# Six group buffers for the bias, w_out's first words loaded in two earlier places, and their conversion spread over twelve slots

## The chip, the cores and the metric

The kernel runs on one core of a Trainium2 chip. The metric is the device time of one execution in microseconds; lower is better. A run's number is the median of several executions.

## The reference

Three layers are computed one after the other. The first is attention over 4 batches and 8 heads with 576 positions of 64 numbers, with a bias per pair of positions that a small network computes from the positions alone:

```python
scores = scale * np.matmul(q, k.transpose(0, 1, 3, 2))
x = (psi_rel / psi_i)[..., None]
h = np.maximum(x @ w1 + b1, 0.0)
bias = h @ w2
scores = scores + bias.transpose(2, 0, 1)[None, :, :, :]
...
attn = np.exp(scores)
attn = attn / (np.sum(attn, axis=-1, keepdims=True) + 1e-09)
return np.matmul(attn, v).astype(np.float32)
```

The second layer is a gated one, `(x @ w1) * (x @ w2) @ w3 @ w_out`, and the third a softmax-weighted one with a layer norm. The weights of the last two layers arrive as 64-bit floats and are made into 32-bit floats on the chip.

## The kernel before

**The bias.** `Bias.run` (L178 on) computes the bias of all heads in 36 groups of 16 query rows. For a group, four masks of 128 rows are made from a table of logarithms (`masks`, L163), about 11 of 16 on ScalarE (L169) and the others on VectorE (L171), two groups ahead. TensorE multiplies them into two PSUM halves (L192, 24 matmuls for a piece of up to 512 columns). VectorE combines the two halves into a row buffer `rs` in SBUF (L202 and L207), GpSimd writes the mirrored part of it (`pool_round`, L54), and SyncE's queue SP writes the buffer to DRAM (`write`, L47, 295.5 KB, shown as `bias_d<-rs`). There are three `rs` buffers (L199), so group n+3 waits in L202 until the write of group n has landed.

After each group, `beside(n)` puts other things between: the first pair's q and k are prepared (`Attention.start`), and bias rows are read back from DRAM for the attention (`load_bias`, shown as `b<-bias_d` and `bt<-bias_d`). At n = 23 the first two of the attention's bias blocks are read, and right after them `load_wo` loads 1 MB of `w_out` (two DMAs of 512 KB, `rwo<-in_wo`). All these DMAs are issued by SP in the order of the code; a write to DRAM stands behind whatever was issued before it.

**The attention.** It works in slots; ten slots make one pair of heads and one batch, and each engine's order in a slot is the order of the code in `slot` (L490 on). In slot s, VectorE adds the bias to the scores of block k of slot s-1 (`add_bias`, L389), takes reciprocals (L405) and makes the second half of transposed blocks (L512); ScalarE takes exponentials (L396) two slots behind and copies transposed blocks (L496); GpSimd adds to the sums (L403), normalises (L409), and splits the next pair's q, k and v into high and low parts (L54 and L57); TensorE makes scores (L376), transposes (L419) from slot 8 on, and values (L462) from slot 11 on. SP copies q and k into place for the next pair (`q<-qh`, `k<-kr`, L51).

**w_out's conversion.** `f64_steps` (L64 on) turns 64-bit words into floats in five steps: one on ScalarE (L69) and four on VectorE (L70 to L73). `first_wo` makes two such chains, each with a DMA at its end (`big<-wo`), twelve steps in all, in the order a1 b1 a2 b2 and so on. `FILL` (L223) says how many of them are taken at the end of which slot: two in slot 3, eight in slot 4, two in slot 5. The other parts of w_out are converted by `conv_wo`, thirteen slots for each (`wx`, `wraw`).

Of the kernel before, what the change touches and what calls it, by code (L numbers as in the profile page):

```python
# [7 lines left out]
F = mybir.dt.float32  # L8
B = mybir.dt.bfloat16
R = mybir.dt.float32r  # L10
U = mybir.dt.uint32
# [6 lines left out]
S = 576  # L18
# [65 lines left out]
class Bias:  # L84
# [93 lines left out]
    def run(self, beside):  # L178
        nc = self.nc
        order = list(range(32, 36)) + list(range(32))  # L180
        mq = [self.masks(g) for g in order[: self.AHEAD]]
        for n, g in enumerate(order):
            w, r = self.width(g), 16 * g + 15
            mk = mq.pop(0)
            pieces = [(0, w)] if w <= 512 else [(0, w // 2), (w // 2, w // 2)]
            made = []
            for at, ln in pieces:
                ps = self.pp.tile([128, 2, 512], F, tag="ps", name="ps")
                for ab in range(2):
                    for part in range(3):  # L190
                        for q in range(4):
                            nc.tensor.matmul(  # L192
                                ps[32 * q : 32 * q + 32, ab, :ln], self.cb[:, part, ab], mk[q][:, at : at + ln],
                                start=part == 0, stop=part == 2, tile_position=(0, 32 * q),
                            )
                made.append(ps)
            if n + self.AHEAD < len(order):
                mq.append(self.masks(order[n + self.AHEAD]))
            rs = self.wp.tile([128, 2 * S], F, tag="rs", name="rs", bufs=3)  # L199
            for (at, ln), ps in zip(pieces, made):  # L200
                to = rs[:, r + at : r + at + ln]
                nc.vector.scalar_tensor_tensor(  # L202
                    out=to, in0=self.lt[:, at : at + ln], scalar=self.ip16[:, g : g + 1], in1=ps[:, 0, :ln], op0=ALU.mult, op1=ALU.mult
                )
            for (at, ln), ps in zip(pieces, made):
                to = rs[:, r + at : r + at + ln]
                nc.vector.tensor_tensor(out=to, in0=to, in1=ps[:, 1, :ln], op=ALU.add)  # L207
            self.ch.pool_round(rs[:, :r], rs[:, r + 1 : 2 * r + 1][:, ::-1])
            self.write(g, rs)
            beside(n)  # L210
        nc.scalar.activation(self.warm, self.warm, AF.Exp)


class Attention:
# [5 lines left out]

    LAG = 8
    AVLAG = 2
    FILL = {3: 2, 4: 8, 5: 2}  # L223

    def __init__(self, ch, i, bias, x_d, ga):
        self.ch, self.nc, self.i = ch, ch.nc, i
# [23 lines left out]
        self.tps = ch.pool(self.psr, "atp", "right", bufs=2, space=PSUM)  # L250
        self.ops = ch.pool(self.psr, "aop", "right", bufs=1, space=PSUM)

    def load_wo(self):

        for f in range(2):
            self.ch.load(self.ga.raw_wo[:, f], self.i["wo"].bitcast(U)[f * 128 : f * 128 + 128])

    def first_wo(self):

# [230 lines left out]
    def slot(self, s):  # L490
# [33 lines left out]
        if n < NP:  # L524
# [19 lines left out]
            if s == 0:  # L544
                self.fill = self.first_wo()
            for _ in range(self.FILL.get(s, 0)):
                self.fill.pop(0)()
# [505 lines left out]
def tile_kernel(tc, i, out):  # L1053
    with tc.manual_schedule(), tc.tile_pool(name="dram", bufs=1, space=DRAM) as dp:
        x_d = [dp.tile([2, DM, S], F, name="x_d%d" % b) for b in range(NB)]
        x2_d = [dp.tile([DM, TC], F, name="x2_d%d" % c) for c in range(NC)]
        gw_d = dp.tile([FF, DM], F, name="gw_d")
        ch = Chip(tc)

        ga = Gated(ch, i, x_d, x2_d, gw_d)  # L1060
        ga.open_keep()
        bias = Bias(ch, i, dp)
        bias.open()
        at = Attention(ch, i, bias, x_d, ga)
        at.open_left()

        def beside(n):

            at.start(n)
            if n == 7:  # L1070
                at.load_bias(0, 0)
            if n == 23:
                at.load_bias(0, 1, 2)
                at.load_wo()
            if n == 26:
                at.load_bias(0, 5, 6)
            if n == 29:
                at.load_bias(0, 3)
                at.load_bias(0, 7)

        bias.run(beside)
        at.load_bias(0, 4)
        at.load_bias(0, 8)
        bias.ctx.close()
        at.open_right()
        scored = 10 * len(at.pairs)
        for s in range(at.slots()):
            n = s - scored
            if n == 0:
                at.left.close()  # L1090
                at.psl.close()
                ga.open_left()
            if n == ga.MID:
                at.top.close()
                ga.open_mid()
            at.slot(s)
            ga.early(n)
        at.right.close()
        at.psr.close()
        ga.open_right()  # L1100
        ga.run()
        ga.right.close()
        ga.psr.close()
        so = Solu(ch, i, ga, out)
        so.open()
        so.run()
        so.ctx.close()
        ga.left.close()
        ga.psl.close()
# [62 lines left out]
```

## Time and profile before

| | us |
|---|---|
| median of 3 runs | 978.24 |
| lowest and highest run | 974.11, 980.3 |
| the profiled execution's own time | 973.8 |
| its span, first to last instruction | 972.0 |

TensorE (PE) is busy 893.5 us of the span, VectorE (DVE) 602.2, ScalarE (ACT) 495.6 and GpSimd (POOL) 414.4. The mean granted TensorE clock is 0.979 of full speed. Times in the trace count from the span's start: the bias phase fills the first 84 us, the attention runs to about 400 us, and the two other layers fill the rest.

### The profile page before, as it was taken

The numbers are of one execution on the slowest core, as the hardware profiler recorded it, in microseconds if no ns is written. First come the engines' busy times: TensorE is split into PE (matmuls) and PEld (weight loads), VectorE is DVE, ScalarE is ACT, GpSimd is POOL, SyncE is SP. The second block draws the span as 40 slices with busy tenths as digits, with TensorE's granted clock in tenths as the row PEclk, the third lists the DMA queues.
The fourth block names the chain that finished last, engine by engine and source line by source line (L and its number), as shares of the span: only waits on it lengthen the run. The fifth ranks groups of instructions, "written<-read, shape, count | busy, mean of one in ns | idle before, by whom it ended". The sixth has DMA issues, their size and how long they took to land.

```text
span 972.0 us, 16454 instructions
## 1 busy us (share of the span) xinstructions
PE 893.5 (92%) x5890; PEld 792.3 (82%) x5890; DVE 602.2 (62%) x1292; ACT 495.6 (51%) x1018; POOL 414.4 (43%) x536
## 2 busy tenths in 40 slices
PE   5666999999989996799899999999999999999998
PEld 4334888888888885688799999999999888888886
DVE  7878889888888888899915656230111644444442
ACT  8974888788787886454423432332222333233222
POOL 3125887887877863010203657572322221022000
PEclk9987999999999998899999999999999999999999
DMA  4767789789789674555404252502110211111000
GB/s 139 252 226 215 210 219 276 212 233 288 191 227 304 178 194 147 160 191 178 157 18 159 74 192 87 178 18 86 35 65 24 62 49 55 31 46 55 22 23 33
DMA packets 83842, 133.76 MB, mean 138 GB/s; under 512 B 14896, under 2 KB 47536, under 8 KB 83760
## 3 DMA queue, kind: packets, MB, share of 16 engines
q1 hardware_dynamic: 83616, 132.40, 44.9%
q8 instruction: 47, 0.77, 0.3%
q10 hardware_dynamic: 144, 0.29, 0.1%
q14 instruction: 35, 0.29, 0.1%
HBM read 71.44 MB, written 31.86 MB: 106 GB/s over the span
## 4 chain that ended last, share of the span: by engine, by line
PE 57%; DVE 17%; POOL 9%; DMA 7%; issue 5%; ACT 3%; SPq 2%; POOLq 0%; DVEq 0%; ACTq 0%
PE ab L81 9%; PE ab L80 9%; PE ab L79 9%; PE o L81 3%; PE o L80 3%; PE o L79 3%; PE x L81 3%; PE x L80 3%; PE x L79 3%; PE op L462 2%; PE tp L419 2%; DVE e L389 2%; PE sp L376 2%; DVE etl L512 2%; PE ps L192 2%
## 5 line engine op out<-in xcount | busy, mean ns | idle before, releaser
L79 PE MATMUL ab<-xh,ab 128*128 128x384 f32 x384 | 130.8, 341 | 7.4 <-ACT ab L661 7.0
L81 PE MATMUL ab<-xh,ab 128*128 128x384 f32 x384 | 130.3, 339 | 0.9 <-DVE ab L664 0.9
L80 PE MATMUL ab<-xl,ab 128*128 128x384 f32 x384 | 130.4, 340 | 0.4 <-DVE xl L735 0.4
L771 DVE TENSOR_TENSOR a<-ab,a 128x384 f32<-128x384 f32 x48 | 26.7, 556 | 134.8 <-ACT a L770 134.8
L409 POOL TENSOR_SCALAR e<-e,st 128x576 f32<-128x576 f32 x128 | 96.2, 760 | 28.0 <-DVE st L405 27.0
L62 POOL TENSOR_TENSOR gl<-a,gh 128x384 fp32r<-128x384 f32 x40 | 46.0, 1150 | 142.2 <-ACT gh L61 142.2
L419 PE MATMUL tp<-idt,e 128*128 128x128 f32 x576 | 89.4, 278 | 18.6 <-DVE etl L512 15.4
L376 PE MATMUL sp<-k,q 128*128 128x288 f32 x512 | 95.8, 312 | 10.5 <-DVE st L389 8.3
L396 ACT ACTIVATE e<-e,st 128x576 f32<-128x576 f32 x128 | 100.0, 782 | 8.1 <-DVE st L389 7.9
L496 ACT CAST eth<-tp 128x512 fp32r<-128x512 f32 (+1 forms) x160 | 85.1, 543 | 35.9 <-PE tp L419 33.2
L512 DVE TENSOR_TENSOR etl<-tp,eth 128x512 fp32r<-128x512 f32 (+1 forms) x160 | 99.1, 627 | 5.3 <-ACT eth L496 4.3
L389 DVE CUSTOM_DVE_ANT_0 e<-sp,bt 128x576 f32<-128x576 f32 x128 | 95.4, 746 | 1.7 <-PE sp L376 1.7
L376 PEld LDWEIGHTS sp<-k,q 128*128 128x128 f32 x512 | 76.0, 194 | 19.4 <-DVE st L389 11.8
L419 PEld LDWEIGHTS tp<-idt,e 128*128 128x128 f32 x576 | 66.9, 141 | 28.8 <-DVE etl L512 13.2
L984 DVE TENSOR_REDUCE st<-ab 128x1 f32<-128x1024 f32 x18 | 22.0, 1224 | 107.8 <-PE ab L81 107.8
L1004 POOL TENSOR_TENSOR st<-st,half 128x1 f32<-128x1 f32 x18 | 9.9, 549 | 176.0 <-DVE st L1003 176.0
L79 PEld LDWEIGHTS ab<-xh,ab 128*128 128x128 f32 x384 | 73.1, 190 | 9.2 <-ACT ab L661 7.6
L770 ACT COPY a<-ab 128x384 f32<-128x384 f32 x48 | 22.9, 478 | 111.5 <-PE ab L81 96.1
L192 PE MATMUL ps<-mk,cb 128*32 128x264 bf16 (+17 forms) x1056 | 53.2, 347 | 27.4 <-DVE mk L171 18.0
L81 PEld LDWEIGHTS ab<-xh,ab 128*128 128x128 f32 x384 | 72.9, 190 | 2.3 <-DVE ab L664 2.3
L80 PEld LDWEIGHTS ab<-xl,ab 128*128 128x128 f32 x384 | 73.1, 190 | 1.5 <-DVE xl L735 1.3
L192 PEld LDWEIGHTS <-cb 128*32 128x32 bf16 x1056 | 32.7, 104 | 47.4 <-issue 23.9
(164 smaller groups left out, 2310.7 us busy)
## 6 DMA issues: line engine op xcount, KB each, us to landing
bias_d<-rs SPq DMA_DIRECT2D x36, 295.5 KB, 2.7
qkr<-in_qk SPq DMA_DIRECT2D x16, 608.0 KB, 4.6
k<-kr SPq DMA_DIRECT2D x32, 288.0 KB, 4.2
x_d<-o SPq DMA_DIRECT2D x64, 144.0 KB, 4.1
k<-kr SPq DMA_DIRECT2D x32, 256.0 KB, 4.2
raw<-in_w SPq DMA_DIRECT2D x16, 512.0 KB, 4.5
raw<-in_w3t SPq DMA_DIRECT2D x16, 512.0 KB, 4.1
vr<-in_v SPq DMA_DIRECT2D x16, 288.0 KB, 4.4
```

The costliest lines, as they stand in the source:

```text
L62: (eng or self.nc.gpsimd).tensor_tensor(out=lo, in0=x, in1=hi.bitcast(F), op=ALU.subtract)
L79: mm(out, a[0], b[0], start=first, stop=False)
L80: mm(out, a[0], b[1], start=False, stop=False)
L81: mm(out, a[1], b[0], start=False, stop=last)
L192: nc.tensor.matmul(ps[32 * q : 32 * q + 32, ab, :ln], self.cb[:, part, ab], mk[q][:, at : at + ln], start=part == 0, stop=part == 2, tile_ ...
L376: nc.tensor.matmul(ps[:, half, :HS], w["q"][:, h, q * 128 : q * 128 + 128], w["k"][:, h, x, half * HS : half * HS + HS], start=x == 0, sto ...
L389: self.nc.vector.tensor_tensor_reduce(out=halves(e), in0=ps[:, :, :HS], in1=halves(self.BT[(self.pairs[n][0], k)]), scale=-0.125, scalar=3e38,
L396: self.nc.scalar.activation(e, e, AF.Exp, bias=st[:, c : c + 1], scale=-1.0, accum_out=st[:, 2 + c : 3 + c])
L409: self.nc.gpsimd.tensor_scalar(out=e, in0=e, scalar1=st[:, c : c + 1], scalar2=1.0, op0=ALU.mult, op1=ALU.mult)
L419: tr = lambda c, src: nc.tensor.transpose(ps[: src.shape[1], c * 128 : c * 128 + 128], src, self.idt)
L496: self.nc.scalar.copy(hi, src)
L512: self.nc.vector.tensor_tensor(out=lo, in0=src, in1=hi.bitcast(F), op=ALU.subtract)
```

## The change

Three things are changed. The tag `rs` gets six buffers in place of three. `load_wo` takes one half at a time and is called after group 10 and after group 16 (the 11th and the 17th), no longer twice after group 23. `FILL` takes one of the twelve steps in each of the slots 0 to 11.

```diff
-            rs = self.wp.tile([128, 2 * S], F, tag="rs", name="rs", bufs=3)
+            rs = self.wp.tile([128, 2 * S], F, tag="rs", name="rs", bufs=6)
...
-    FILL = {3: 2, 4: 8, 5: 2}
+    FILL = {s: 1 for s in range(12)}
...
-    def load_wo(self):
+    def load_wo(self, f):
 
-        for f in range(2):
-            self.ch.load(self.ga.raw_wo[:, f], self.i["wo"].bitcast(U)[f * 128 : f * 128 + 128])
+        self.ch.load(self.ga.raw_wo[:, f], self.i["wo"].bitcast(U)[f * 128 : f * 128 + 128])
...
+            if n in (10, 16):
+                at.load_wo(n // 16)
             if n == 23:
                 at.load_bias(0, 1, 2)
-                at.load_wo()
```

On SP's queue, in the last two thirds of the bias phase, this stood before (`bias_d_74` and `bias_d_75` are two of the three DRAM areas of the bias, `rwo` is w_out's raw words, `bt` a bias block for the attention):

```order
L51 DMA k<-kr 64x2x64
L47 DMA bias_d_74<-rs 128x591 x3
L47 DMA qkr<-in_qk 128x1216
L47 DMA bias_d_74<-rs 128x591 x5
L47 DMA bias_d_75<-rs 128x591 x4
L47 DMA bt<-bias_d_74 128x2x576
L47 DMA rwo<-in_wo 128x1024 x2
L47 DMA bias_d_75<-rs 128x591 x3
```

Now there stands:

```order
L47 DMA rwo<-in_wo 128x1024
L47 DMA bias_d_74<-rs 128x591
L51 DMA k<-kr 64x2x64
L47 DMA bias_d_74<-rs 128x591 x3
L47 DMA qkr<-in_qk 128x1216
L47 DMA bias_d_74<-rs 128x591 x2
L47 DMA rwo<-in_wo 128x1024
L47 DMA bias_d_74<-rs 128x591 x3
L47 DMA bias_d_75<-rs 128x591 x4
L47 DMA bt<-bias_d_74 128x2x576
L47 DMA bias_d_75<-rs 128x591 x3
```

The two loads have moved ahead of 13 and 7 bias writes, and the three writes after the first `bt` read follow it directly.

On VectorE, from the add of block 3 of the first pair in slot 4 (`e,st<-sp,bt` is an add of the bias, `wo` the words in conversion), this stood before:

```order
L389 ISA e,st<-sp,bt 128x576
L389 ISA st 128x1
L405 RECIPROCAL st<-st 128x2
L70 TENSOR_SCALAR wo<-wo 128x512 x2
L71 TENSOR_SCALAR wo<-wo 128x512 x2
L72 SCALAR_TENSOR_TENSOR wo<-rwo,wo 128x512 x2
L73 SCALAR_TENSOR_TENSOR wo<-rwo,wo 128x512 x2
L389 ISA e,st<-sp,bt 128x576
```

From the same add on there now stands (lines of the attention have numbers one less than before; the two steps of L70 stand in the two slots ahead):

```order
L388 ISA e,st<-sp,bt 128x576
L388 ISA st 128x1
L404 RECIPROCAL st<-st 128x2
L71 TENSOR_SCALAR wo<-wo 128x512
L388 ISA e,st<-sp,bt 128x576
L388 ISA st 128x1
L71 TENSOR_SCALAR wo<-wo 128x512
L388 ISA e,st<-sp,bt 128x576
L388 ISA st 128x1
L404 RECIPROCAL st<-st 128x2
L72 SCALAR_TENSOR_TENSOR wo<-rwo,wo 128x512
L388 ISA e,st<-sp,bt 128x576
```

The eight steps in a row have become one step between each two adds; the adds of blocks 4 and 5 no longer stand behind all of them.

## Rows read from the trace of the kernel before

**Rows 1.** Stages (us, busy time of PE, PEld, DVE, ACT, POOL, PEclk, DMA share, GB/s)
```profile
100.00:125.00 25.00, 23.77 (x168) 20.98 (x169) 21.31 (x59) 20.72 (x51) 21.13 (x31) 1.00 0.69 192
...
500.00:600.00 100.00, 99.81 (x576) 99.49 (x575) 52.71 (x76) 35.02 (x70) 50.92 (x43) 1.00 0.36 122
```

**Rows 2.** What L202 waited for in the first 100 us (us, times)
```profile
  DMA bias_d<-rs: 5.5, 2
```

**Rows 3.** Timeline, 59 to 70 us (start, us, engine, instruction [idle before <- releaser])
```profile
59.14 0.99 SPq L47 DMA_DIRECT2D rwo<-in_wo  x2
...
60.17 2.75 SPq L47 DMA_DIRECT2D bias_d<-rs  x3
...
67.93 0.61 DVE L202 SCALAR_TENSOR_TENSOR rs<-lt,con,ps 128x384 f32<-128x384 f32 x1 [5.13 <-DMA bias_d<-rs]
...
69.60 8.84 PE L192 MATMUL ps<-mk,cb 128*32 128x432 bf16 x119 [5.50 <-DVE mk L171]
```

**Rows 4.** DMAs issued from L47 between 60 and 61.5 us (two bias writes)
```profile
DMA to landing us min/median/max: 7.3/7.5/7.6
```

**Rows 5.** Stretches around the stall and the start of the attention, columns of rows 1
```profile
62.80:67.93 5.13, 1.30 (x24) 0.60 (x23) 0.00 (x1) 4.04 (x7) 0.00 (x0) 1.00 1.01 356
67.93:82.12 14.19, 11.30 (x148) 6.20 (x147) 13.04 (x23) 6.68 (x9) 4.86 (x7) 0.76 0.60 211
82.12:89.30 7.18, 4.83 (x20) 3.93 (x20) 4.48 (x13) 4.43 (x10) 5.74 (x7) 0.76 0.54 190
89.30:94.35 5.05, 0.00 (x0) 0.00 (x0) 5.05 (x8) 0.00 (x0) 3.80 (x4) 0.80 0.98 248
```

**Rows 6.** ScalarE's masks after 57 us, timeline
```profile
57.52 9.32 ACT L169 ACTIVATE mk<-lt,nb,scb 128x400 bf16<-128x400 f32 x14 [0.60 <-PE ps L192]
71.69 3.69 ACT L169 ACTIVATE mk<-lt,nb,scb 128x480 bf16<-128x480 f32 x5 [4.85 <-PE ps L192]
75.85 1.52 ACT L169 ACTIVATE mk<-lt,nb,scb 128x512 bf16<-128x512 f32 x2 [0.46 <-PE ps L192]
```

**Rows 7.** Stretches in which the moved loads are issued now, columns of rows 1
```profile
30.00:40.00 10.00, 6.05 (x112) 2.89 (x108) 8.12 (x15) 9.71 (x16) 2.15 (x5) 1.00 0.88 264
40.00:50.00 10.00, 6.35 (x138) 3.59 (x134) 8.73 (x19) 8.65 (x16) 2.30 (x6) 1.00 0.62 218
```

**Rows 8.** The burst of conversion steps and what stands around it, timeline
```profile
86.69 1.27 SPq L47 DMA_DIRECT2D bt<-bias_d  x3
...
89.13 0.17 DVE L405 RECIPROCAL st<-st 128x2 f32<-128x2 f32 x1 [1.81 <-POOL st L403]
89.22 0.74 DVE L70 TENSOR_SCALAR wo<-wo 128x512 f32<-128x512 f32 x2
...
89.87 1.22 DVE L71 TENSOR_SCALAR wo<-wo 128x512 uint32<-128x512 uint32 x2
...
94.35 0.74 DVE L389 CUSTOM_DVE_ANT_0 e<-sp,bt 128x576 f32<-128x576 f32 x1
...
95.16 3.51 PE L376 MATMUL sp<-k,q 128*128 128x288 f32 x12 [6.45 <-DVE st L389]
```

**Rows 9.** DMAs issued from L47 between 86.6 and 88 us (three bias reads)
```profile
DMA to landing us min/median/max: 2.8/3.0/3.6
```

**Rows 10.** VectorE from the burst to the add of the second pair's first block, columns of rows 1
```profile
89.30:103.09 13.79, 7.52 (x40) 6.61 (x41) 11.86 (x29) 6.35 (x17) 10.17 (x14) 0.75 0.97 264
```

**Rows 11.** GpSimd beside the burst and later, timeline
```profile
90.47 1.15 POOL L409 TENSOR_SCALAR e<-e,st 128x576 f32<-128x576 f32 x1
...
92.77 0.51 POOL L403 TENSOR_SCALAR st<-st 128x2 f32<-128x2 f32 x1
...
104.33 0.74 POOL L409 TENSOR_SCALAR e<-e,st 128x576 f32<-128x576 f32 x1 [0.29 <-DVE st L405]
```

**Rows 12.** L72 in the whole span, by tile (ns min/median/max)
```profile
L72 DVE SCALAR_TENSOR_TENSOR cm<-raw,cm x48: 672/686/1826, 371.1 to 606.4; 128x512 uint32<-128x512 uint32 x48
...
L72 DVE SCALAR_TENSOR_TENSOR wo<-rwo,wo x2: 1145/1145/1145, 91.0 to 92.1; 128x512 uint32<-128x512 uint32 x2
```

## The prediction

> **What bounds the kernel now.** I read the busy times by stretch first, because the share of TensorE over the span hides where it waits. In the long middle of the attention TensorE is busy 23.77 of 25 us, and in the layers behind it 99.81 of 100 [rows 1]: there nothing of this change is felt, and a time saved ahead of it is carried to the end whole. What can be won lies in the first 105 us. The view of one line's waits comes next: in the first 100 us the combining step L202 stood idle 5.5 us, twice, for a write of a group's buffer [rows 2]. The timeline shows the large one of the two: at 67.93 VectorE had been idle 5.13 us, until a bias write landed, and TensorE behind it 5.50 us, until VectorE had made its next mask [rows 3]. That write had been issued among three at 60.17, right behind the two 512 KB loads of w_out's words [rows 3], and the writes issued there took about 7.5 us to land [rows 4], in a stretch in which the DMA engines are busy all the time (share 1.01) [rows 5]. With three buffers, group n waits for the write of group n-3, and some 1.5 us a group gives such a write under 5 us.
>
> The second place is the burst of conversion steps. After a reciprocal at 89.13 VectorE does eight steps, from 89.22 to 94.35; the add of block 4 comes only then, and TensorE starts at 95.16 after 6.45 us of idleness [rows 8]. In 89.30 to 94.35 TensorE and ScalarE do nothing, VectorE is full (5.05 of 5.05), and GpSimd works 3.80 us [rows 5].
>
> **The change part by part, against the profiled execution (973.8 us with its span of 972.0; 4.4 under the median of the runs shown).**
>
> *Six buffers and the moved loads.* They have one answer: the stall of 5.13 us. Either alone would take most of it: the loads leave the queue ahead of the writes, and six buffers give a write of 7.5 us some 9 us (six groups of 1.5). What is late next? In 67.93 to 82.12, the last nine groups, VectorE is busy 13.04 of 14.19 us, at a granted clock of 0.76 for TensorE [rows 5], which ran at the lower of its two levels, 1.2 GHz, for a part of it, after the 5.50 us of idleness. So VectorE is next, and beyond the 5.13 us at most 1.15 us of its idle time are left. ScalarE doesn't come ahead of it: the 21 masks that it still had to make at 57.52 take 9.32 + 3.69 + 1.52 = 14.53 us [rows 6], so they can be ready at 72.1, and VectorE, free of stall and idle time, reaches the last group at 82.12 - 5.13 - 1.15 = 75.8. I take 5.13 and most of the 1.15 (0.9, since the clock's fall follows the idleness and the small wait for a write goes with the buffers): **6.0 us, between 3.3 and 6.3**. The low end is the case in which the DMA engines are next, below.
>
> *What the loads cost in their new place.* They add 512 KB each to 30 to 40 and to 40 to 50 us, where the DMA share is 0.88 and 0.62 [rows 7]. At 264 GB/s one is 2.0 us of all engines. SP is delayed by the issue, 0.99 us for both [rows 3]. The bias writes and the copies of the first pair's k behind them land up to 2 us later. I cost this at nothing: the six buffers hide it, and the first pair's k is not read before the attention starts, behind the last stretch of the bias at 82.12 us [rows 5]. Without that cover it would be up to 2 us each, 4 in all.
>
> *The conversion in twelve slots.* The same twelve steps remain, so VectorE does no less; only idle time can be won. Were every step out of the way, the add of block 4 could follow at 89.30 and the gain would be 5.05 us; its data would just be there: the bias read of block 4, first of three issued at 86.69, lands after 2.8 to 3.6 us [rows 8, 9], at 89.5 to 90.3. But the steps come back between the adds. From 89.30 to 103.09, the first add of the second pair, VectorE is busy 11.86 of 13.79 us [rows 10]. Idle are 1.93 us; the two steps of L70 (0.74) [rows 8] now stand in slots 2 and 3, in 82.12 to 89.30, where VectorE is busy only 4.48 of 7.18 us [rows 5]. So VectorE alone allows 1.93 + 0.74 = 2.67 us at that add. One new wait stands against it: in slot 6 the reciprocal needs GpSimd's sum, which ended at 92.77 + 0.51 = 93.28 [rows 11], while VectorE, with two adds and two steps of L71 (0.61 each) [rows 8], is there at about 89.30 + 2 x 0.7 + 2 x 0.61 = 91.9 (an add is 0.74 with its overlap) [rows 8]. GpSimd's instructions beside the burst are the slow ones, 1.15 us for a normalisation that takes 0.74 elsewhere [rows 11]; with fewer conversions beside them they end earlier, so of this 1.4 us wait I take half, 0.7. Behind that waiting reciprocal stand the L72 step and the adds of slot 7 on, and TensorE's score buffers wait for these. **2.67 - 0.7 = 2.0 us**, between 0 (every won gap comes back as a wait for GpSimd) and 5.05 (later waits for GpSimd go too). The ScalarE steps in slots 0 and 1 cost nothing: it is busy 4.43 of 7.18 us there [rows 5]. The two writes back of the converted words now stand behind the load of v on SP; SP can wait there for slot 9's last step, with the next pair's q and k copies behind it, which need GpSimd's later parts anyway.
>
> *Port shared by VectorE and GpSimd.* A step of L72 on 512 columns takes 672 ns at its least, but 1145 in both steps of the burst, and up to 1826 [rows 12], and a GpSimd normalisation 1.15 in place of 0.74 beside it [rows 11]: each slows the other. The Trainium skill (SBUF — State Buffer, Who interferes with whom) says that a VectorE instruction with two SBUF inputs and a GpSimd one that reads SBUF hold the shared port in turn, the second one being blocked for the first's whole length. By that rule scattered steps meet more GpSimd instructions than one burst did, and the second part's gain would go; by rows 10 it is 2.0 us. What the loss would be stands below as a rival, from rows.
>
> **Sum.** 6.0 + 2.0 = 8.0 us: 965.8 for such an execution, and against the median 978.24 - 8.0 = **970.2 us**. Its own range is 967 to 973, from 6 + 5 and 3.3 + 2 us.
>
> **The rivals.**
>
> *A. The burst was a wait for the whole chain (967.1 us).* Then the 5.05 us go whole, with 6.0 from the bias: 978.2 - 11.1. For it: no engine but VectorE and GpSimd works in the burst [rows 5]. Against it: VectorE is 86% busy in the slots around it [rows 10], and in the steady part 21.31 of 25 us [rows 1].
>
> *B. Scattered steps block and are blocked (974.2 us).* Each of the eight VectorE steps loses 0.47 us (1145 less 672 ns [rows 12]) against a GpSimd instruction: 3.8 us. The burst's two L72 steps paid 0.94 of this already at least, so up to 2.8 are new, and 6.0 + 2.0 - 2.8 = 5.2 us are left; GpSimd's own loss (0.41 in a normalisation [rows 11], in some three of them 1.2) on top leaves 4.0. For it: both engines slow each other in the burst [rows 11, 12]. Against it: GpSimd was there 75% busy already (3.80 of 5.05 [rows 5]), so the burst had paid most of it.
>
> *C. The DMA engines are next in the bias phase (972.9 us).* 62.80 to 67.93 shows them full at 356 GB/s [rows 5]. The traffic of 62.80 to 82.12 is 5.13 x 356 + 14.19 x 211 kB, 4.8 MB. In the 13.0 us that VectorE needs, this would be 370 GB/s; taking out the two loads, largely done by 67, leaves 4.0 MB or 300. If 240 GB/s (248 in the late burst stretch [rows 5]) is all that the mix of rows allows, they need 16.6 us, 2.7 less than 19.3: 2.7 to 3.3 us in place of 6.0, with 2.0 from the slots.
>
> *D. The last bias read comes late (slower, 981.0 us).* One place: SP's queue from the last write on. If the compressed phase leaves the DMA engines with a backlog, the last write lands no earlier than now, at about 86.5, so the bias part gives nothing; and the bias read of block 4 then takes 7.5 us [rows 4] in place of 2.8 [rows 9], 4.7 more, with the q and k copies of the next pair behind it. 4.7 - 2.0 = 2.7 us slower. It decides from the point where the share of the DMA engines stays at 1 up to the end of the phase; today it is 0.60 and 0.54 in the two stretches there [rows 5], which speaks against it.
>
> **How the numbers follow.** The forecast has 0.5; A 0.2, B 0.12, C 0.12, D 0.06. The range leaves out little beyond the ends of A and B, with the 3 us by which runs of one kernel differ: 965 to 976. About 1%, 9.8 us, is what a measurement of this kernel can tell from no change. A lies past it mostly, and of the forecast the part with later gains: 0.2 x 0.75 + 0.5 x 0.25 = 0.27 for faster. D stays within 1%; a bad pair of runs leaves 0.02 for slower, and 0.71 for the same.
>
> **What would show it.** Right: L202 shows no wait for a bias write over 1 us; the last bias group's L202 starts at 76 to 77 us, not at 82.12; the add of block 4 comes about 10 us earlier than 94.35, but the second pair's first add only 8 us earlier than 103.09; the granted clock of the last bias groups is higher than 0.76. Wrong: L202 still waits for a write (C); the wait for the sums grows, with L72 steps well over 1.2 us (B); the bias reads after the last write land in over 6 us (D); or the start comes 8 us earlier and the end doesn't, because the layers behind wait for something else.

## The result and the profile after

The changed kernel takes 962.81 us (median of 4 runs, 961.74 to 965.65) against 978.09 us for the kernel before in the same rounds (974.11 to 980.3). The ratio is 0.986, with a 95% interval of 0.9834 to 0.9887: 1.4% faster, where the forecast was 970.2 and "no change" by 1% the likeliest. The sign and the two places were right, the size was too small, and the measured median lies below the range.

The profiled executions differ by less than the medians: 962.9 us after (0.1 over its median) against 973.8 before (4.3 under its median), 10.9 us. The page of the kernel after, its span, busy times and the chain that ended last:

```profile
span 961.1 us, 16446 instructions
...
PE 894.2 (93%) x5890; PEld 793.6 (83%) x5890; DVE 603.1 (63%) x1292; ACT 495.2 (52%) x1018; POOL 415.1 (43%) x536
...
PE 57%; DVE 18%; POOL 9%; DMA 6%; issue 5%; ACT 4%; SPq 1%; POOLq 0%; ACTq 0%; DVEq 0%
```

No engine's busy time differs by more than 0.9 us from before; what went is idle time. The stretches of the kernel after, with the columns of [rows 1]; the first is the last nine bias groups, the second the first pair's first slots, the third its slots up to the second pair [rows 5, 10], the last two to [rows 1]:

```profile
60.47:73.59 13.12, 10.90 (x171) 5.19 (x170) 12.85 (x25) 11.97 (x18) 4.70 (x7) 1.00 0.86 287
73.59:80.80 7.21, 3.63 (x20) 2.81 (x20) 6.27 (x13) 3.25 (x7) 6.00 (x6) 1.00 0.59 213
81.45:93.29 11.84, 8.72 (x35) 7.84 (x35) 9.43 (x27) 6.60 (x17) 10.29 (x14) 0.50 0.98 265
100.00:125.00 25.00, 23.52 (x171) 21.00 (x170) 21.82 (x58) 21.19 (x52) 20.55 (x30) 1.00 0.85 214
500.00:600.00 100.00, 99.81 (x575) 99.49 (x574) 59.05 (x82) 34.23 (x70) 58.66 (x48) 1.00 0.37 127
```

The last nine groups, 14.19 us long before, take 13.12, with VectorE busy 12.85 of them: it is the bound now. The granted clock there is 1.00 in place of 0.76; the idleness of 5.50 us that came ahead of the fall [rows 3] is gone. The clock is at the lower level (0.50) later, from the add of block 4 to the second pair, where GpSimd is the busiest (10.29 of 11.84 us). In the last two stretches TensorE is about as busy as before [rows 1].

What VectorE does around the end of the bias phase and in the first pair's slots, timeline of the kernel after:

```profile
73.59 0.74 DVE L202 SCALAR_TENSOR_TENSOR rs<-lt,con,ps 128x512 f32<-128x512 f32 x1
...
76.64 1.80 DVE L70 TENSOR_SCALAR wo<-wo 128x512 f32<-128x512 f32 x1
78.36 0.74 DVE L388 CUSTOM_DVE_ANT_0 e<-sp,bt 128x576 f32<-128x576 f32 x1
...
81.05 0.17 DVE L404 RECIPROCAL st<-st 128x2 f32<-128x2 f32 x1 [0.93 <-POOL st L402]
81.13 0.41 DVE L71 TENSOR_SCALAR wo<-wo 128x512 uint32<-128x512 uint32 x1
81.45 0.75 DVE L388 CUSTOM_DVE_ANT_0 e<-sp,bt 128x576 f32<-128x576 f32 x1
...
84.07 0.17 DVE L404 RECIPROCAL st<-st 128x2 f32<-128x2 f32 x1 [0.81 <-POOL st L402]
...
88.36 0.17 DVE L404 RECIPROCAL st<-st 128x2 f32<-128x2 f32 x1 [1.55 <-POOL st L402]
...
93.29 0.74 DVE L388 CUSTOM_DVE_ANT_0 eab<-sp,b 128x576 f32<-128x576 f32 x1
```

The last L202 starts at 73.59, not 82.12: 8.5 us earlier. The add of block 4 (the second L388 shown here) comes at 81.45 in place of 94.35 [rows 8], 12.9 earlier, but the second pair's first add at 93.29 in place of 103.09, 9.8 earlier: the burst is gone, and waits of the reciprocals for GpSimd's sums have come back for it, as the forecast had it.

I follow five points in every kernel (us from the start of the span). The end of the bias phase is the start of the last L202; the next are the second pair's first add and the attention's 20th and 140th add (attention adds counted from 0 as in the traces), then the end of the span:

| kernel | last L202 | second pair | add 20 | add 140 | end |
|---|---|---|---|---|---|
| before | 82.12 | 103.09 | 123.88 | 353.71 | 972.0 |
| before, once more | 82.89 | 104.02 | 124.65 | 356.33 | 975.2 |
| after | 73.59 | 93.29 | 113.92 | 341.72 | 961.1 |
| after, once more | 73.70 | 93.37 | 114.15 | 344.78 | 963.9 |

By the means of two profiles each, 8.9 us are won up to the end of the bias phase, 1.4 from there to the second pair, nothing more up to add 20, and 1.5 from there to add 140. That last number is smaller than the scatter of one kernel (229.8 and 231.7 us before, 227.8 and 230.6 after). Behind add 140 0.7 us are lost again, so that the ends are 11.1 us apart. So the bias term was sized too small (6.0), the slot term about right (2.0), and some 4 us of the medians' 15.3 show in no stage of these profiles. (The interval above reaches from 11 to 16 us.)

The bias phase shows where its part comes from. From the 17th L202 (27.25 us before, 29.47 after) to the last, with the columns of [rows 1], before and then after:

```profile
27.25:82.12 54.87, 36.98 (x628) 20.29 (x627) 44.04 (x86) 43.56 (x70) 14.18 (x26) 0.91 0.71 235
```

```profile
29.47:73.59 44.12, 34.24 (x628) 17.47 (x627) 43.19 (x87) 42.97 (x71) 14.13 (x26) 1.00 0.88 287
```

VectorE's work is nearly the same, and its idle time falls from 10.83 to 0.93 us. These 10.7 us are won there; ahead of it 2.2 are lost.

### The profile page after: what moved, and what is told of

It reads as the page before. It is cut to its first block, busy times and chain, and to the rows that moved or that the text cites. A ratio compares the mean times of both kernels' runs of the same rounds, so it can differ in the third digit from the quotient of the medians.

```text
span 961.1 us, 16446 instructions
## 1 busy us (share of the span) xinstructions
PE 894.2 (93%) x5890; PEld 793.6 (83%) x5890; DVE 603.1 (63%) x1292; ACT 495.2 (52%) x1018; POOL 415.1 (43%) x536
## 4 chain that ended last, share of the span: by engine, by line
PE 57%; DVE 18%; POOL 9%; DMA 6%; issue 5%; ACT 4%; SPq 1%; POOLq 0%; ACTq 0%; DVEq 0%
PE ab L81 9%; PE ab L80 9%; PE ab L79 9%; PE o L81 4%; PE o L80 4%; PE o L79 4%; PE x L80 3%; PE x L79 3%; PE x L81 3%; PE op L461 2%; PE tp L418 2%; DVE etl L511 2%; DVE e L388 2%; DVE mk L171 2%; PE sp L375 2%
## 5 line engine op out<-in xcount | busy, mean ns | idle before, releaser
L388 DVE CUSTOM_DVE_ANT_0 e<-sp,bt 128x576 f32<-128x576 f32 x128 | 95.4, 745 | 0.2 <-PE sp L375 0.2
L192 PE MATMUL ps<-mk,cb 128*32 128x264 bf16 (+17 forms) x1056 | 51.5, 331 | 21.1 <-DVE mk L171 10.5
L725 POOL TENSOR_TENSOR xs<-xh,xl 128x384 f32<-128x384 f32 x24 | 27.2, 1140 | 92.6 <-DMA xl<-x_d 58.4
```

Of the source, the lines that this page charges most:

```text
L192: nc.tensor.matmul(ps[32 * q : 32 * q + 32, ab, :ln], self.cb[:, part, ab], mk[q][:, at : at + ln], start=part == 0, stop=part == 2, tile_ ...
L388: self.nc.vector.tensor_tensor_reduce(out=halves(e), in0=ps[:, :, :HS], in1=halves(self.BT[(self.pairs[n][0], k)]), scale=-0.125, scalar=3e38,
```

## The experiments

All kernels were timed against the kernel before in five rounds. Four questions: which of the three edits carries the gain; why the bias part gave more than the waits named for a DMA; whether blocking between VectorE and GpSimd costs something; and where the scatter in the attention comes from.

### One edit at a time

Before once more, and before with one of the three edits each:

```diff
# six_only                            # loads_only: load_wo split, after groups 10 and 16
-    ... name="rs", bufs=3)           # fill_only
+    ... name="rs", bufs=6)           +    FILL = {s: 1 for s in range(12)}
```

> The kernel before once more, unchanged, for a second profile of it and its scatter. Theory T (L202's idle time before a group is nearly all waiting for the write of the group three earlier to land, also where the rows named TensorE or GpSimd: 9.9 us in the profile of before, not 5.5): each L202 that sat idle over 0.15 us from group 7 on starts 0.05 to 0.15 us after the landing of the write three groups earlier, again in this profile; if its time is near the median 978, the idle time before L202 is longer than 9.9 us by about as much as it is slower than 973.8. Rival R (the rows' names are right, and the scatter of before comes from elsewhere): the idle time named for TensorE has no landing just ahead of it, and the scatter lies behind 105 us.

> Six buffers alone; the loads stay behind group 23 and the conversion stays a burst. Theory T: all waits of L202 for writes go, 7 to 10 us in the first 84 us, and the time is 964 to 971 us. Rival R: only the 5.5 us named for DMA go, and L202 keeps 3 to 4 us of waits for TensorE: 971 to 974 us.

> The two loads moved, alone; three buffers and the burst stay. Theory T: the stall at the 28th group shrinks to 1 or 2 us, but the loads put their 2 us each ahead of other writes, for which three buffers have no room, so that L202 waits 1 to 3 us there; the sum of its waits stays over 5 us and the time is 973 to 979 us. Rival R: the stall was the loads' doing, and 4 to 5 us go: 972 to 974 us.

> The conversion spread over twelve slots, alone; three buffers and the loads behind group 23 stay. Theory T: the second pair's first add comes 1 to 2 us earlier against the end of the bias phase, and the time is 1 to 2 us lower than before, which its scatter may hide. Rival (the burst was a wait for the whole chain): 5 us lower.

| kernel | median us (before 979.16) | ratio, 95% interval | last L202 | second pair | end |
|---|---|---|---|---|---|
| before_again | 978.0 | 0.9996, 0.9975 to 1.0017 | 82.89 | 104.02 | 975.2 |
| six_only | 970.24 | 0.9916, 0.9893 to 0.9939 | 73.95 | 95.08 | 970.5 |
| loads_only | 976.8 | 0.9983, 0.9967 to 1.0 | 82.69 | 103.80 | 975.1 |
| fill_only | 977.81 | 0.9996, 0.9981 to 1.0012 | 84.59 | 104.31 | 973.3 |

The buffers carry the change: they alone end the bias phase at 73.95, with one wait for a write left (1.47 us, shown in the last section). The forecast said that either alone, buffers or moved loads, would take most of the stall. For the loads that was of no use: with the loads moved and three buffers the phase ends at 82.69. The waits of L202 in loads_only, first 100 us, say why:

```profile
  DMA bias_d<-rs: 8.2, 6
  PE ps L192: 2.6, 4
  POOL rs L54: 0.3, 1
```

The long wait of 5.13 us is down to 2.40 (in its timeline), and the other waits for a write are longer (1.62, 1.71 and 1.17 us the next largest): the writes are late in several places, not behind the two loads alone. One of the waits put down to TensorE (1.02) and the one put down to GpSimd end behind the landing of a write, too, so that 9.5 us of such waits are left. That led back to the kernel before. Beside the 5.5 us of [rows 2], its L202 waited from 30 to 84 us for:

```profile
  PE ps L192: 3.3, 3
  POOL rs L54: 1.0, 3
```

The three waits put down to TensorE, on VectorE's timeline of before:

```profile
34.67 0.70 DVE L202 SCALAR_TENSOR_TENSOR rs<-lt,con,ps 128x464 f32<-128x464 f32 x1 [1.32 <-PE ps L192]
...
47.56 0.58 DVE L202 SCALAR_TENSOR_TENSOR rs<-lt,con,ps 128x352 f32<-128x352 f32 x1 [0.93 <-PE ps L192]
...
54.59 0.53 DVE L202 SCALAR_TENSOR_TENSOR rs<-lt,con,ps 128x304 f32<-128x304 f32 x1 [1.10 <-PE ps L192]
```

The bias writes of three groups earlier were issued at 30.6, 44.0 and 51.1 us; the issues of L47 at these three times, before:

```profile
L47 SPq DMA_DIRECT2D bias_d<-rs x1: 553/553/553, 30.6 to 30.6; - x1
...
DMA to landing us min/median/max: 4.0/4.0/4.0
...
L47 SPq DMA_DIRECT2D bias_d<-rs x1: 319/319/319, 44.0 to 44.0; - x1
...
DMA to landing us min/median/max: 3.5/3.5/3.5
...
L47 SPq DMA_DIRECT2D bias_d<-rs x1: 320/320/320, 51.1 to 51.1; - x1
...
DMA to landing us min/median/max: 3.3/3.3/3.3
```

30.6 + 4.0 = 34.6, 44.0 + 3.5 = 47.5, 51.1 + 3.3 = 54.4: each L202 starts 0.1 to 0.2 us behind the landing of the buffer it needs. These waits too ended with a write, and so did the three put down to GpSimd: by the trace's exact times all eight L202 start 0.12 us behind the landing of the write three groups earlier. Together they are 5.5 + 3.3 + 1.0 = 9.8 us. The second profile of before names most such waits for what they are (L202, first 100 us, before_again; the groups are partly others, and one more wait, 0.83 us, is put down to TensorE and ends 0.12 us behind a landing):

```profile
  DMA bias_d<-rs: 9.8, 7
  PE ps L192: 2.3, 4
```

That makes 10.6 us, 0.7 more than in the first profile, while the execution took 3.2 us longer: the expectation that the two go together was missed, and the scatter of before lies mostly elsewhere. In the kernel after, this row is all that is left, in the same stretch:

```profile
  PE ps L192: 1.7, 3
```

### Two edits at a time, and four buffers

after_again is the changed kernel; six_loads is it with the FILL of before; six_fill is it with load_wo where it was; four_bufs has `bufs=4` in place of 6.

> The changed kernel once more, unchanged. Theory S (part of the gain over 9.8 us is scatter of the attention's later pairs, where GpSimd's qh step waits for the next pair's q and k load: 7.0 us of such waits after 95 us in the first profile of the changed kernel, 9.2 to 11.9 in the others): a second profile has 9 to 12 us of them and a median of 965 to 968 us. Theory D (the changed kernel has fewer of these waits in every run): 6 to 8 us of them again, and a median of 962 to 965 us.

> Six buffers and the moved loads; the conversion stays a burst. Theory S: the moved loads add little to six buffers, and the time is that of six buffers alone, 968 to 971 us. Theory D with the loads as its cause: 963 to 966 us. In both the bias phase ends within 0.7 us of the changed kernel's.

> Six buffers and the conversion in twelve slots; the loads stay behind group 23. Theory S: six buffers and 1 to 2 us more, 967 to 970 us. Theory D with the spread conversion as its cause: 963 to 966 us.

> The changed kernel with four buffers in place of six. A write landing 5.8 us after its issue at most needs room for about four groups of 1.5 us: with four buffers L202 waits 1 to 3 us in all (against 0 with six and 8 to 10 with three), so that 964 to 967 us come out if the writes' landing times set the wait, and the changed kernel's time if one buffer more is enough. Rival (only the loads behind group 23 needed room): no wait at all.

| kernel | median us (before 978.14) | ratio, 95% interval | last L202 | second pair | end |
|---|---|---|---|---|---|
| after_again | 963.72 | 0.9847, 0.9819 to 0.9875 | 73.70 | 93.37 | 963.9 |
| six_loads | 965.66 | 0.9866, 0.9841 to 0.9892 | 71.99 | 92.98 | 965.5 |
| six_fill | 965.41 | 0.9864, 0.9839 to 0.9888 | 73.05 | 92.73 | 965.2 |
| four_bufs | 969.07 | 0.9896, 0.987 to 0.9922 | 76.62 | 96.30 | 967.3 |

With the loads moved, the number of buffers is a dose: 9.5 us of waits for a write with three (loads_only), 3.9 with four, none with six. Four buffers were expected to leave 1 to 3 us and a time of 964 to 967 us; they leave more. With six buffers and the loads where they were, one wait is left (1.47 us in six_only, 0.93 in six_fill). L202 in four_bufs:

```profile
  DMA bias_d<-rs: 3.9, 3
  PE ps L192: 1.0, 2
```

One of six_loads and six_fill was expected to carry what six_only lacks (963 to 966 us) and the other not; both carry it. Taken off the whole change, the conversion's place and the loads' place are each worth 1.7 to 1.9 us, with intervals that overlap; the last set below prices them with less scatter. six_loads ends its bias phase 1.6 us ahead of after, where 0.7 at the most was expected; the next part shows why that can be.

### What the first groups and the slots give back

Two things in the kernel after are dearer than in before. First, its 17th L202 starts at 29.47 us and not at 27.25: 2.2 us of the bias gain are lost before the first long wait (the second profiles have 28.14 and 29.57). VectorE's masks and GpSimd's instructions there, timeline of after:

```profile
18.18 1.85 DVE L171 TENSOR_SCALAR mk<-lt,scl,nb 128x544 bf16<-128x544 f32 x1
...
21.53 1.69 DVE L171 TENSOR_SCALAR mk<-lt,scl,nb 128x528 bf16<-128x528 f32 x1
...
18.18 1.55 POOL L57 TENSOR_TENSOR ql<-qkr,qh 128x640 fp32r<-128x640 f32 x1
...
21.51 1.42 POOL L57 TENSOR_TENSOR kr<-qkr,kr 128x576 fp32r<-128x576 f32 x1
```

In before the 128x544 mask takes 0.91 us. Both long masks start with a subtraction of GpSimd and end just behind it. In quarters that subtraction of the first pair is cut into four pieces:

```diff
-            ch.pool_rest(w["ql"], qr, w["qh"])
+            for c in range(0, 640, 160 if n == 0 else 640):
+                d = slice(c, c + (160 if n == 0 else 640))
+                ch.pool_rest(w["ql"][:, d], qr[:, d], w["qh"][:, d])
```

(and the same for `kr`, in pieces of 144). Second, GpSimd's sums: no_steps leaves VectorE's eight conversion steps out altogether. And since VectorE is the bound of the last bias groups now, more_act gives ScalarE one more of 16 masks there:

```diff
-            chains.append(self.ch.f64_steps(...) + [out])            # no_steps
+            steps = self.ch.f64_steps(...)
+            chains.append(steps[:1] + [lambda: None] * 4 + [out])
-            if (self.no * self.ON_ACT) % 16 < self.ON_ACT:           # more_act
+            on_act = self.ON_ACT + (self.no >= 72)
+            if (self.no * on_act) % 16 < on_act:
```

The fourth, q_early, is on the scatter, below.

> The changed kernel with GpSimd's two long subtractions for the first pair (1.4 to 1.6 us each, in the bias phase) cut into four pieces each. Theory P (a VectorE mask that is issued while such a subtraction runs is held until it ends, 1.85 and 1.69 us in place of 0.45 to 0.5, the 2.2 us which the changed kernel loses at groups 5 to 12): no mask takes over 1.1 us, the 17th L202 starts 1 to 2.2 us earlier than at 29.5, and the bias phase ends 0.5 to 2 us earlier. Rival (the long masks come from elsewhere): they stay over 1.5 us.

> The changed kernel without the eight VectorE steps of w_out's first two conversion chains (L70 to L73); the words written back are then not w_out. It shows what the spread steps still cost. If VectorE alone sets the first slots, their 5 us come off the second pair's first add; if GpSimd and the bias reads do, as the waits for its sums (0.9, 0.8 and 1.55 us in the first slots) say, 0 to 2 us do, and the median stays within 2 us of the changed kernel's.

> The changed kernel with 12 instead of 11 of 16 masks on ScalarE in the second half of the bias phase. With no wait for a write left, VectorE is without idle time from 12.5 to 74 us there and ScalarE ends its last mask 3.8 us ahead of the last L202; some four masks of 0.5 us move over, so that the phase ends 1 to 2 us earlier, if VectorE is the bound; if ScalarE is close behind it, 0 to 0.5 us.

| kernel | median us (before 978.51) | ratio, 95% interval | last L202 | second pair | add 20 | end |
|---|---|---|---|---|---|---|
| quarters | 963.81 | 0.9859, 0.9836 to 0.9882 | 74.19 | 93.92 | 114.65 | 966.3 |
| no_steps | 965.55 | 0.9867, 0.9848 to 0.9885 | 72.44 | 89.56 | 113.03 | 963.9 |
| more_act | 963.87 | 0.9854, 0.9835 to 0.9873 | 72.72 | 92.41 | 113.56 | 963.4 |

In quarters no mask is held for the length of a whole subtraction (the two that meet pieces of 0.5 us take 0.78 and 0.74), and the 17th L202 starts at 27.33. Not all of these 2.1 us are the cut's: the 544 mask ends at 18.59, and the first subtraction starts only at 19.08. In no_steps, where the subtractions are whole, the first one starts at 19.16 by chance; its 544 mask takes 0.56 us, its 512 mask 1.58, and its 17th L202 starts at 28.28. The time isn't lower in quarters: its groups ran into a wait that the kernel after doesn't have. Timeline of quarters, whose profiled execution is the slowest of its five (968.06 us; the second row is L202 behind a write issued at 38.2, right behind a moved load, which landed 7.6 us later):

```profile
17.74 0.85 DVE L171 TENSOR_SCALAR mk<-lt,scl,nb 128x544 bf16<-128x544 f32 x1
...
45.84 0.60 DVE L202 SCALAR_TENSOR_TENSOR rs<-lt,con,ps 128x368 f32<-128x368 f32 x1 [2.80 <-DMA bias_d<-rs]
```

So a moved load can cost something with six buffers too: this write was issued 5.1 us behind its group's L202 (2.9 in after), which left it 4.9 us (7.0 in after). That the faster groups made the difference isn't shown; six_loads is nearly as early (27.86) and has no such wait. In no_steps the second pair starts 3.7 us earlier than in after, 1.2 of them because its bias phase ended earlier, and by add 20 only 0.9 of the 3.7 are left. What the reciprocals waited for, about 75 to 100 us, in after and then in no_steps:

```profile
  POOL st L402: 4.2, 5
```

```profile
  POOL st L403: 7.8, 5
```

Without the eight steps, VectorE waits 3.6 us more for GpSimd. But 2.42 us of the 7.8 are one wait behind the second pair's first add, and GpSimd was late there because it had itself waited for a load, on the timeline of no_steps:

```profile
91.69 0.73 POOL L54 TENSOR_SCALAR qh<-qkr 128x640 fp32r<-128x640 f32 x1 [2.33 <-DMA qkr<-in_qk]
...
92.73 0.16 DVE L405 RECIPROCAL st<-st 128x1 f32<-128x1 f32 x1 [2.42 <-POOL st L403]
```

So against the end of the bias phase the second pair gains 2.6 us without the steps, and the load of the next q and k takes them back. Whether the steps could be placed better once that load comes earlier (below) isn't shown. more_act ends the bias phase 1 us earlier, and the median shows none of it. None of the three tells a version that beats the kernel after.

### The scatter in the attention

The lowest and the highest run of before_again are 10 us apart (975.35 and 985.52), and add 20 to add 140 takes 227.8 to 231.7 us. In most pairs GpSimd's first step (L54, `qh`) waits for the load of the next pair's q and k, which is issued in slot 5 behind other work of SP. One line of the view of tile `qh`, in before, after, and after_again (2.7, 2.2 and 2.2 us of it are one wait in the bias phase):

```profile
  DMA qkr<-in_qk: 7.5, 5
```

```profile
  DMA qkr<-in_qk: 5.8, 4
```

```profile
  DMA qkr<-in_qk: 6.9, 4
```

This names a part of them only. Over all `qh` steps that stood idle after 95 us, whatever name their wait has, I count 9.2 and 10.4 us in the two profiles of before, 7.0 and 9.8 in those of after, and 9.6 to 11.9 in the other kernels of the first three sets; in before, after and after_again each of them starts 0.14 to 0.24 us behind the landing of its load. The first profile of after alone looked as if the change made the load land in time; the second says no, though its median (963.72) stays. q_early gives q its own tile, with two buffers, and loads it five slots earlier:

```diff
+        w["qr0"] = self.qk.tile([128, 640], F, tag="qr0", name="qr0", bufs=2)
+        self.ch.load(w["qr0"], self.i["qk"][b, p][:, :640])
...
-            if k == 5 and n + 2 < NP:
+            if k == 0 and n + 2 < NP:
```

(k is loaded into a tile `kr0` in slot 5 as before.) With the same edit on the kernel before (before_q), and on six_only, six_loads and six_fill (six_q, six_loads_q, six_fill_q), the change can be priced again without these waits.

> The changed kernel with the next pair's raw q and k in two tiles of their own, the q part with two buffers and loaded five slots earlier. Theory W (the attention's scatter of 2 to 5 us from run to run, and 7 to 12 us of GpSimd's idle time, are waits of the qh step for the load of q and k, issued behind six copies of k): these waits fall under 2 us, the stretch from the 20th to the 140th add shrinks from 228 to 231 us to 224 to 227, and the median is 957 to 962 us. Rival (TensorE is the bound there and GpSimd's waits are hidden, or the earlier load takes its time from the copies): 962 to 966 us.

> The kernel before with the early q load of q_early and nothing of the change. Theory S (the scatter and a part of the measured 15 us lie in the waits for the q and k load, which the change doesn't touch): 965 to 969 us, so that the change is worth 10 to 12 us here (its stage sum from the profiles: 8.9 in the bias phase, 1.4 up to the second pair's first add). Theory D (the change is worth 15 us): 969 to 972 us.

> Six buffers and the early q load; loads and burst as before. Theory S: 1 to 4 us over q_early's 955.2 (a write behind the two loads still lands later than six groups, 1.5 us, and the burst's 1.4 us): 956 to 959 us. Theory D: 960 to 963 us, 5 to 7 over q_early as six_only is over the changed kernel.

> Six buffers, the moved loads and the early q load; the burst stays. Theory S: within 2 us of q_early, 955 to 957 us. Theory D: 957 to 960.

> Six buffers, the spread conversion and the early q load; the loads stay behind group 23. Theory S: within 2 us of q_early, 955 to 957 us, with one wait of about 1 us for a write behind the loads. Theory D: 957 to 960.

| kernel | median us | ratio to before, 95% interval | last L202 | second pair | add 20 | end |
|---|---|---|---|---|---|---|
| before_q | 968.65 | 0.9878, 0.9855 to 0.9901 | 85.03 | 106.14 | 125.89 | 966.8 |
| six_q | 958.01 | 0.9779, 0.9755 to 0.9802 | 73.12 | 94.24 | 114.01 | 955.5 |
| six_loads_q | 957.59 | 0.9768, 0.9745 to 0.9791 | 71.41 | 92.53 | 112.30 | 955.8 |
| six_fill_q | 955.83 | 0.9756, 0.9732 to 0.978 | 73.04 | 92.73 | 112.45 | 955.7 |
| q_early | 955.19 | 0.9762, 0.9741 to 0.9782 | 73.18 | 92.88 | 112.64 | 953.8 |

(before was 978.51 beside q_early and 979.26 beside the other four.) six_loads_q lies 0.6 us above the range that was expected, and in six_fill_q L202 waits for no write, where one wait of about 1 us was. After 95 us no such wait is left in q_early, whose one wait of `qh` stands in the bias phase:

```profile
  DMA qr<-in_qk: 1.9, 1
```

q_early beats both kernels, by more than the 957 us that was the best expected, and its runs lie between 952.62 and 955.7. With the edit on both sides the change is worth 968.65 - 955.19 = 13.5 us by the medians (10 to 12 were expected), and here the profiled spans say nearly the same, 966.8 - 953.8 = 13.0: 11.85 up to the last L202, 1.4 to the second pair, and nothing behind it. The two medians come from different rounds, though, in which before differs by 0.75 us; by the two ratios to before (0.9878 and 0.9762) the change is worth 11.4 us. Six buffers alone are worth 10.6 us; with them the conversion adds 2.2 and the moved loads 0.4, all in the same rounds, and both together 2.8 (2.1 with the 0.75 taken off). At add 20 the same kernels are 11.9 (buffers), 13.4 (with the conversion), 13.6 (with the loads) and 13.3 us (both) ahead of before_q: the buffers' share is plain, and how the other 1.5 to 3 us divide isn't settled, since the intervals of these kernels overlap. The waits of L202 in before_q, first 100 us, are close to the price of the buffers, in part by luck (six_q keeps one such wait, 1.46 us, and starts its 17th L202 1.8 us earlier):

```profile
  DMA bias_d<-rs: 10.7, 6
  PE ps L192: 1.4, 3
```

## Why the prediction was wrong

**The bias term (6.0 us, measured 8.9 and 11.9): the step that failed.** The term was mis-sized, and the failing step is the price taken from the row of L202's waits [rows 2]: "the combining step L202 stood idle 5.5 us, twice, for a write". The other 4.3 us of L202's idle time named TensorE or GpSimd, and I took them for what they said. They ended 0.12 us behind a write's landing, and six buffers took them as well. The forecast's measure of a write's room, "some 1.5 us a group gives such a write under 5 us", hid them: it counts three groups from L202 to L202, but a write is issued only 1.6 to 3.3 us behind the L202 of its group. In the eight waits 2.4 to 3.9 us were left, and writes that landed in 3.3 to 4.0 us were late, too. (Six buffers likewise left 7.35 us and not the forecast's 9 for the write behind the loads in six_only, which took 8.7.) From the 17th L202 on, 10.7 us were won in the profile of after; 2.2 were given back ahead of it, most of them at the two blocked masks. In before_q and q_early the two masks are long on both sides (1.56 and 1.69 us, 1.58 and 1.69), the 17th L202 starts at 29.21 and 29.03, and nothing is given back: 11.9 remain.

**Either alone.** Nearly right for the buffers: six_only keeps 1.47 us of such waits. Wrong in effect for the loads: loads_only takes 2.7 of the 5.13 us, but 9.5 us of waits for a write stay, and so does the time (0.9983).

**What is late next.** Right: VectorE, busy 12.85 of 13.12 us, and the clock at 1.00 there. ScalarE doesn't come first: more_act gave it more without harm, and without gain.

**The moved loads cost nothing.** Right for the change as it stands (the intervals of six_fill and after_again overlap), with less room than I gave it: in quarters a write behind the same load made a wait of 2.80 us.

**The slots (2.0 us, measured 1.4).** Right in size and in reason: the add of block 4 was to come about 10 us earlier and the second pair's only 8; it was 12.9 and 9.8. The wait for GpSimd's sum in slot 6 is there (0.81 us at 84.07, 0.7 taken); over the five reciprocals from the first one to the one behind the second pair's first add, such waits grew from 3.0 to 3.5 us. With three buffers the same edit shows nothing in the time (0.9996), though the way from the last L202 to the second pair is 19.7 us in its profile and 21.0 and 21.1 in those of before; with six and q early it shows 2.2 us, with intervals that overlap.

**Rival A** (the burst was the whole chain) falls: against the end of the bias phase the second pair came 1.4 us earlier and not 5.05, and even in no_steps, without the eight steps, only 3.9 us. **Rival C** and **D** fall: the DMA engines carry 287 GB/s in the last nine groups without holding VectorE, and the last three bias reads land as before [rows 9], after 2.8, 3.1 and 2.8 us; issues of L47 from 78 to 81 us in after, these reads and two other loads:

```profile
DMA to landing us min/median/max: 2.8/3.1/4.4
```

**Rival B** is there at one step of eight. The L70 step at 76.64 takes 1.80 us, against 0.74 for the two of the burst together [rows 8], beside a GpSimd subtraction:

```profile
76.60 1.55 POOL L57 TENSOR_TENSOR ql<-qkr,qh 128x640 fp32r<-128x640 f32 x1
```

Its 1.4 us are mostly hidden, since the reciprocal behind it waits for GpSimd even so (0.93 at 81.05); it starts 7.5 us behind the last L202, and 7.0 in no_steps. In return the L72 steps go from 1.145 [rows 12] to 0.69 us, as the row of after shows, and all eight steps take 5.83 us in place of 5.77:

```profile
L72 DVE SCALAR_TENSOR_TENSOR wo<-rwo,wo x2: 669/693/717, 84.2 to 85.4; 128x512 uint32<-128x512 uint32 x2
```

The Trainium skill (SBUF — State Buffer, Who interferes with whom) counts `tensor_scalar`, which this step and the masks are, among the VectorE operations that can contend with GpSimd, and says that whichever issues first holds the shared ports for its whole instruction while the other is blocked. Here the trace agrees: the step and the two masks above start 0 to 0.04 us behind GpSimd's subtraction and end 0.3 us behind it. In before the 544 mask started 0.57 us ahead of the subtraction and took 0.91 us; there the subtraction is the longer one (1.73). I had weighed the rule for two SBUF inputs at the conversion steps alone; its toll was taken at masks in the bias phase.

**The baseline.** The range began at 965, some 2 us under its lowest rival (967.1), for scatter. The median of before stands 4.3 us over its profiled execution, and the sum from that execution was put on the median without asking what made the two differ. The runs with the early load point to the waits for q and k as a part of that scatter: in the five kernels that have it, the four or five runs of each lie within 1.2 to 3.7 us, in the others with four to six runs within 2.2 to 6.4. Why the medians differ by 15.3 us and the profiled spans by 10.9 and 11.3 stays open; the runs that weren't profiled can't be looked into, and with these waits out of the way the difference is 11.4 (by the ratios) to 13.5 us (by the medians) in the times and 13.0 in the spans.

## What to carry to other kernels

A wait for several semaphores carries one name only. Where a buffer is reused after a DMA, put the landing of that DMA beside the start of each instruction that reuses it, and price the buffers from all waits that end there, whatever name they have; a second profile of the same kernel may name them otherwise. A buffer count is a dose (9.5, 3.9 and 0 us for three, four and six here, with the loads moved), and the time from a write's issue to the reuse of its buffer, not from one reuse to the next, has to be above the landing time of the slowest write, not of the usual one. Before scatter is taken as noise, look for a load on which an engine in order waits round after round: moved five slots earlier, into a tile with two buffers, it took 8.5 us off the kernel after (963.72 to 955.19) and 10.6 off the kernel before (979.26 to 968.65).

## What the runs showed of the hardware

A mask of 128x544 that takes 0.56 us in no_steps and 0.91 in before took 1.85 when it started together with a GpSimd subtraction of 1.55, and an L70 step of 0.4 us took 1.80: the blocked one pays nearly the whole length of the other. And a write lands later right behind loads on its queue (whether by its place there or because the DMA engines are full isn't separated): in after the write at 38.05, behind a load, took 6.2 us and the one at 35.89, ahead of it, 3.5; in six_only the three writes issued from 56.7 us on stand behind the two loads of 512 KB at 55.69, and the first took 8.7 us, where the three writes shown for before took 3.3 to 4.0. Issues of L47 at 56.2 and 56.7 in six_only (the load and the write):

```profile
DMA to landing us min/median/max: 8.3/8.5/8.7
```

VectorE still waited 1.47 us for it with six buffers, a wait that the trace put down to TensorE once more:

```profile
65.52 0.66 DVE L202 SCALAR_TENSOR_TENSOR rs<-lt,con,ps 128x432 f32<-128x432 f32 x1 [1.47 <-PE ps L192]
```
